# Scores of q as two column tiles of 64 tokens, with k's scores and v's products placed beside them

## The chip, the cores and the metric

The kernel runs on one core of a Trainium2 chip. The metric is device time of one execution in microseconds (us), the median of several runs; a change of about 0.2% (2.2 us) is the least that a measurement of this kernel tells from none.

## What is computed

Agent attention over 12,480 tokens of 128 channels with 49 agents, and behind it two feed-forward layers of width 2048. Everything is float32; the weights of the layers arrive as 64-bit floats and are split into two float32 parts on the chip.

```python
def _attn_ref(q, k, v, agents):
    scale = 1.0 / np.sqrt(q.shape[-1])
    def sm(a, b):
        s = scale * (a @ b.transpose(0, 2, 1))
        s = s - s.max(-1, keepdims=True)
        e = np.exp(s)
        return e / (e.sum(-1, keepdims=True) + 1e-09)
    a2k = sm(agents, k)
    agent_v = a2k @ v
    q2a = sm(q, agents)
    return (q2a @ agent_v).astype(np.float32)
def reference(...):
    x = attn_out.reshape(B * S, D)
    h = x @ w_in;   x = (h / (1 + exp(-h))) @ w_out
    h = x @ w2_in;  return (h * cos(h)) @ w2_out
```

## The kernel before

There are two stages. The **attention stage** goes over 13 blocks of tokens, numbered 0 to 12: twelve of 1024 tokens (128 partitions by 8) and a last one of 192 (96 by 2). The **feed-forward stage** goes over 25 tiles of up to 512 tokens, four groups of hidden channels each.

In the attention stage the order of all work on all engines is written out by hand, in the tables `ORDER` and `FIRST`: a list of steps, each a function and a block number. Every engine takes its own instructions in that order. `qS3` is `qS(3)`, the scores of q for block 3. The steps that matter here:

- `kT`, `qT` (function `turn`, L267): eight transposes of a block of k or q on TensorE into a double bank of PSUM; `kX`, `qX` (L286): ScalarE copies them to an SBUF tile `xT`, of which there are two.
- `kS` (L303): scores of k. The 64 columns of `agk` (49 agents, padded) are the stationary operand, and 512 tokens stream. Two such matmuls stand side by side in the array as column tiles, at `tile_position` (0, 0) and (0, 64). VectorE takes them away in `kM`.
- `qS` (L379): scores of q. Here 128 tokens are the stationary operand, and `agT` streams, the 49 agents twice, 98 columns; the second 49 are written over by the next matmul. Eight matmuls for a block. VectorE then takes the maximum (`qM`, L388), subtracts it (`qB`, L396); ScalarE does the exponential (`qE`), VectorE the sum (`qZ`, L407).
- `qt` (L440): four transposes of half a block of the packed probabilities into the one bank `y2`; `qk` (L445): ScalarE copies that bank to SBUF, and the next `qt` waits for it.
- `vE` (L337, ScalarE): exponentials of k's scores, two blocks at a time; `vt` (L346): their transposes; `vc` (L352): ScalarE's copy; `va` (L366): their product with v, eight matmuls of 49 columns in two column tiles with 128 channels streaming, added up over all blocks in one bank.
- `dA`, `d0` ... `d4`, `dH`, `dL`: the splitting of a piece of weights, on ScalarE (L459, L475) and VectorE (L463 to L498).
- `z0` to `z4`, `c0` ... : after the last `va`, `c0` (L523, VectorE) and `c1` (L526, ScalarE) take the sums away, and a chain of small steps folds them into the first layer's weights. The feed-forward stage starts behind that.

`kS`, `qS` and `vt` share two banks of PSUM (`bank1`), so each of them waits until the one two places ahead of it has been taken away: `kM`, `qB` or `vc`.

Loads of k, q, v and weights are issued by one queue (SP) in the fixed order `LOADS`, each as soon as a buffer of its kind is free (five for k and q, three for v, three for weights); `va` frees v's buffers, `turn` those of k and q, and `d3` those of the weights. A load of 1024 tokens or of a piece of weights is 524,288 bytes.

A float32 matmul that is no transpose shows as two loads and two matmuls in the trace, a transpose as one of each. So `qS` of a full block has 16 matmuls in the trace, `va` 16, `kS` four and `turn` eight.

Of the kernel before, what the change touches and what calls it, by code (L numbers as in the profile page):

```python
# [33 lines left out]


ORDER = """
dA0 d00 d10 kT0 wm3 d20 dH0 d30 kX0 d40 kT1 dL0 kS0 kX1 kT2 kM0 dA1 kS1 kX2 d01 d11 kT3 kM1 dH1 kS2 d21 kX3 d31
kT4 d41 kS3 kM2 kX4 dL1 kT5 dA2 kM3 kS4 kX5 d02 d12 qT0 d22 dH2 d32 kS5 qX0 kM4 kT6 d42 dA3 qS0 kM5 kX6 d03 d13
kT7 dL2 qM0 kS6 kX7 d23 qB0 kT8 dA4 kM6 kS7 kX8 d04 d33 qT1 qE0 d14 dH3 kS8 qZ0 qX1 kM7 kT10 d24 dH4 d43 qS1
kX10 qR0 dL3 qN0 dA5 kM8 kT9 qM1 qP0 qB1 kS10 qK0 qL0 qE1 qT2 kX9 qZ1 d05 qt0.0 qX2 d15 kT11 qR1 d34 qk0.0 qN1  # L40
kS9 dA6 kM10 kT12 d44 kX11 qS2 qP1 kM9 dH5 qK1 d25 qL1 qt0.1 qM2 kS11 qk0.1 qB2 kX12 qt1.0 d35 qE2 qT3 qk1.0 d06
dL4 kS12 qX3 qT4 kM11 d45 dA7 qt1.1 qS3 d16 qX4 d07 kM12 dH6 x0 qZ2 qT5 qk1.1 d17 x1 qR2 qS4 dH7 qM3 qN2 qX5 x2
qP2 qB3 qK2 x3 qT6 qE3 x4 qL2 qM4 vE12 qZ3 qS5 vE0 d26 qR3 dL5 qN3 qX6 qt2.0 qB4 qT7 d27 qE4 qP3 dA8 qZ4 vt1 qK3
qT8 qM5 qk2.0 qL3 qB5 qX7 qt2.1 qR4 d08 qS6 qN4 qk2.1 d36 vc1 qP4 qE5 vt0 vE2 qM6 qT9 qK4 qB6 qL4 qZ5 qt3.0 vc0
d46 va1 qX8 d18 vt3 qk3.0 vt2 d28 vc3 qR5 va0 d37 qN5 vc2 dL6 qE6 qt3.1 va3 qk3.1 qP5 vE4 d47 qT10 qK5 qt4.0 dA9
qZ6 vt4 qL5 dH8 d09 qS7 qk4.0 d38 vc4 dL7 vE8 qt5.0 qS8 qR6 d19 qN6 qk5.0 qM7 dA10 qB7 qt4.1 qX9 d29 vt5 d48 qP6
va2 qk4.1 qM8 qE7 qK6 qB8 va4 qL6 vE6 qZ7 qt5.1 d39 qS9 vc5 dL8 vE10 qR7 d010 qN7 vt6 qM9 qE8 va5 qB9 qP7 vc6 z0
qK7 d110 vt7 dA11 qL7 va6 qk5.1 qZ8 vc7 z1 qt6.0 qX10 z2 d210 vt9 d310 qT11 qk6.0 d011 dH9 d111 qt6.1 qE9 qS10
qR8 d49 qk6.1 qN8 qZ9 dH11 qR9 vc9 qT12 dL9 qP8 qt7.0 dH10 va7 qM10 qX11 qK8 d410 vt10 qN9 qk7.0 va9 qB10 dL10
qE10 qt7.1 qX12 qS11 dA12 qP9 qZ10 qL8 z3 vc10 d012 qk7.1 qK9 vt8 dA13 qM11 qt8.0 qL9 vc8 va10 qB11 qk8.0 d013  # L50
sp0 qS12 qE11 d211 qt9.0 d112 vt11 qk9.0 qR10 va8 z4 qN10 vc11 qM12 qB12 d311 dH12 qt8.1 sp1 vt12 qE12 va11 vc12
qP10 qZ11 qk8.1 qK10 va12 qL10 qt9.1 c0 c1 qZ12 c2 qk9.1 qR12 d411 qN12 c3 qt10.0 c4 c5 st c6 cP0 qP12 d113 cA0
d212 qk10.0 ri0 d312 dH13 d412 qt10.1 cH0 cA1 dL11 qk10.1 dL12 ch0 cl0 cw0 cP3 dA15 cs0 cP2 ch1 d015 cl3 cP1 cH3
cl2 qR11
"""
# [892 lines left out]
```

## Time and profile before

| | |
|---|---|
| time, median of 3 runs | 1079.82 us (1078.44 to 1080.45) |
| span of the profiled execution, first to last instruction | 1076.8 us |
| profiled execution's own time | not listed; the median of the runs is 3.0 us above its span |
| TensorE busy | 1065.2 us, 99% |
| VectorE busy | 964.1 us, 90% |
| ScalarE busy | 909.8 us, 84% |
| GpSimd busy | 504.0 us, 47% |
| HBM read, written | 27.58 MB, 6.39 MB |

The attention stage is the first 94 us, the folding of the sums and the first hidden groups lie between 94 and 146, and the rest is the steady feed-forward stage. A busy TensorE is not one at its peak: matmuls are pipelined, and their durations overlap. What one costs in a row of its kind is read from the chain of work that ended last, which follows starts.

### The profile page before, as it was taken

To read this page: it belongs to the slowest core of one execution; us is meant where nothing else is said; L and a number is where in the kernel's file an instruction comes from. 1 tells how busy PE (TensorE), PEld (TensorE's weight loads), DVE (VectorE), ACT (ScalarE), POOL (GpSimd) and SP (SyncE) were. 2 spreads that over 40 slices of the span, in tenths; PEclk is the share of its full clock that TensorE was granted. 3 is DMA by queue.
4 is the path that set the end of the run, shared out by engine and by line. 5 is a ranking of instruction groups with operands and counts; after the bars stand their busy time and mean duration, and the time that the engine had idled before them with its cause. 6 is when DMAs were issued, how large, how long until landed. Compare 5 with 4: busy or idle time off the path is not lost.

```text
span 1076.8 us, 14174 instructions
## 1 busy us (share of the span) xinstructions
PE 1065.2 (99%) x5267; PEld 841.2 (78%) x5267; DVE 964.1 (90%) x1067; ACT 909.8 (84%) x972; POOL 504.0 (47%) x264
## 2 busy tenths in 40 slices
PE   9999999999999999999999999999999999999997
PEld 5897777777777777777777777777777777788996
DVE  7877999989999999999989998999999999999897
ACT  5888988888888888888888888888888888888876
POOL 0445044554455445544554455445544554455555
PEclk9999999999999999999999999999999999999999
DMA  9963000000000000000000000000000000000000
GB/s 345 344 226 125 9 6 11 6 16 13 4 16 16 1 17 16 1 16 17 10 6 16 12 5 16 13 4 16 17 1 16 16 1 15 15 11 5 12 9 15
DMA packets 66221, 38.68 MB, mean 36 GB/s; under 512 B 52523, under 2 KB 57184, under 8 KB 66152
## 3 DMA queue, kind: packets, MB, share of 16 engines
q1 hardware_dynamic: 65352, 37.68, 11.5%
q8 instruction: 41, 0.67, 0.3%
q14 instruction: 28, 0.23, 0.1%
q10 hardware_dynamic: 800, 0.10, 0.1%
HBM read 27.58 MB, written 6.39 MB: 32 GB/s over the span
## 4 chain that ended last, share of the span: by engine, by line
PE 95%; DVE 2%; ACT 1%; POOL 1%; DMA 1%; issue 1%; SPq 0%; POOLq 0%; DVEq 0%; ACTq 0%
PE y L733 16%; PE y L737 16%; PE y L734 16%; PE h L701 10%; PE h L775 8%; PE h L777 8%; PE h L776 8%; PE h L689 4%; PE h L267 2%; PE h L379 2%; PE h L303 1%; PE y L366 1%; PE y L440 1%; POOL g2l L834 1%; DMA kraw<-in_k_dram 1%; DVE g L816 1%
## 5 line engine op out<-in xcount | busy, mean ns | idle before, releaser
L834 POOL TENSOR_TENSOR g2l<-g,g2h 128x1024 fp32r<-128x1024 f32 (+2 forms) x200 | 465.5, 2349 | 498.7 <-DVE g1l L724 489.0
L799 DVE SCALAR_TENSOR_TENSOR n<-n,h 128x1024 f32<-128x1024 int32 (+3 forms) x202 | 239.0, 1184 | 63.9 <-ACT n L789 50.8
L789 ACT ACTIVATE n<-h,quarter 128x1024 int32<-128x1024 f32 (+3 forms) x202 | 219.8, 1088 | 88.7 <-PE h L777 88.6
L724 DVE TENSOR_TENSOR g1l<-g,g1h 128x1024 fp32r<-128x1024 f32 (+2 forms) x200 | 239.7, 1199 | 9.7 <-ACT g1h L716 4.1
L816 DVE TENSOR_TENSOR g<-n,h 128x1024 f32<-128x1024 f32 (+3 forms) x202 | 238.0, 1179 | 4.0 <-ACT n L808 0.7
L709 ACT ACTIVATE g<-h 128x1024 f32<-128x1024 f32 (+2 forms) x200 | 199.4, 997 | 36.2 <-PE h L701 36.0
L808 ACT ACTIVATE n<-n,halfpi 128x1024 f32<-128x1024 f32 (+3 forms) x202 | 225.6, 1119 | 0.8 <-DVE n L799 0.8
L716 ACT CAST g1h<-g 128x1024 fp32r<-128x1024 f32 (+2 forms) x200 | 204.9, 1025 | 3.2
L825 DVE CAST g2h<-g 128x1024 fp32r<-128x1024 f32 (+2 forms) x196 | 155.5, 794 | 7.5
L733 PE MATMUL y<-g1h,o1h 128*128 128x512 f32 (+2 forms) x400 | 156.4, 391 | 0.1
L733 PE MATMUL y<-g2h,o2h 128*128 128x512 f32 (+2 forms) x400 | 154.9, 387 | 1.1 <-DVE o L856 0.9
L775 PE MATMUL h<-x2h,i2h 128*128 128x512 f32 (+2 forms) x400 | 154.2, 386 | 1.0 <-DVE g L816 1.0
L734 PE MATMUL y<-g2h,o2l 128*128 128x512 f32 (+2 forms) x400 | 154.5, 386 | 0.0
L734 PE MATMUL y<-g1h,o1l 128*128 128x512 f32 (+2 forms) x400 | 154.0, 385 | 0.0
L777 PE MATMUL h<-x2l,i2h 128*128 128x512 f32 (+2 forms) x400 | 153.9, 385 | 0.0
L776 PE MATMUL h<-x2h,i2l 128*128 128x512 f32 (+2 forms) x400 | 153.9, 385 | 0.0
L701 PE MATMUL h<-pT,w2h 128*128 128x512 f32 (+2 forms) x400 | 132.3, 413 | 0.0
L737 PE MATMUL y<-g2l,o2h 128*128 128x512 f32 (+2 forms) x400 | 122.3, 387 | 1.9 <-POOL g2l L834 1.9
L737 PE MATMUL y<-g1l,o1h 128*128 128x512 f32 (+2 forms) x400 | 121.2, 384 | 0.0
L733 PEld LDWEIGHTS y<-g1h,o1h 128*128 128x128 f32 x400 | 75.1, 188 | 21.1 <-DVE x2l L762 7.8
L701 PEld LDWEIGHTS h<-pT,w2h 128*128 128x128 f32 x400 | 67.3, 188 | 30.9 <-issue 23.9
L737 PEld LDWEIGHTS y<-g2l,o2h 128*128 128x128 f32 x400 | 74.9, 188 | 17.7 <-POOL g2l L834 3.1
(140 smaller groups left out, 1092.5 us busy)
## 6 DMA issues: line engine op xcount, KB each, us to landing
...
```

What stands on the lines that cost most here:

```text
L701: nc.tensor.matmul(out=h1s[g, k][:, j, :toks(t)], lhsT=w2h[:, 128 * c:128 * c + 128], rhs=x, start=False, stop=True)
L724: i = v.tensor_tensor(out=gl, in0=f, in1=b32(gh), op=ALU.subtract)
L733: nc.tensor.matmul(out=y, lhsT=wh[:, c, :], rhs=gh[:, j, :], start=(c == 0), stop=False)
L734: nc.tensor.matmul(out=y, lhsT=wl[:, c, :], rhs=gh[:, j, :], start=False, stop=False)
L737: nc.tensor.matmul(out=y, lhsT=wh[:, c, :], rhs=gl[:, j, :], start=False, stop=(c == NCH - 1))
L775: nc.tensor.matmul(out=y, lhsT=i2h[:, c, :], rhs=xh, start=True, stop=False)
L776: nc.tensor.matmul(out=y, lhsT=i2l[:, c, :], rhs=xh, start=False, stop=False)
L777: nc.tensor.matmul(out=y, lhsT=i2h[:, c, :], rhs=xl, start=False, stop=True)
L799: v.scalar_tensor_tensor(out=b32(n)[:, p], in0=n[:, p], scalar=-2.0 * PI, in1=h2s[g, k][:, p], op0=ALU.mult, op1=ALU.add)
L808: sc.activation(out=r[:, p], in_=r[:, p], func=AF.Sin, bias=halfpi)
L816: v.tensor_tensor(out=f[:, p], in0=r[:, p], in1=h[:, p], op=ALU.mult)
L834: i = (v if (g, k) == (NG - 1, 1) else gp).tensor_tensor(out=gl[:, p], in0=f[:, p], in1=b32(gh)[:, p], op=ALU.subtract)
```

## The change

`qS` now makes two matmuls where it made one. Each takes 64 tokens as stationary operand (64 and 32 in the last block) and streams the 49 agents once; the two stand side by side as column tiles at (0, 0) and (0, 64) and write the two halves of the partitions. `agT` holds the agents once, 196 bytes instead of 392, and one copy on VectorE at the start goes. The tiles that are allocated behind `agT` on its side of SBUF (the split weights, `pT`, `g1`, `g1h`, `g1l`, `x2h`, `x2l` among them) begin 192 bytes lower.

```diff
-    agT = const.tile([128, 2, NA], F32, name="agT")
+    agT = const.tile([128, NA], F32, name="agT")
...
-        for j in range(2):
-            nc.vector.tensor_copy(out=agT[:, j, :], in_=pa[:, :NA])
+        nc.vector.tensor_copy(out=agT, in_=pa[:, :NA])
...
             ps = bank1()
-            ag2 = agT.rearrange("p j a -> p (j a)")
             for i in range(n):
-                nc.tensor.matmul(
-                    out=ps[:p, NA * i:NA * i + 2 * NA], lhsT=xt[:, i // h, p * (i % h):p * (i % h) + p], rhs=ag2,
-                    start=True, stop=True,
-                )
+                for x in range(0, p, 64):
+                    w = min(64, p - x)
+                    at = p * (i % h) + x
+                    nc.tensor.matmul(
+                        out=ps[x:x + w, NA * i:NA * i + NA], lhsT=xt[:, i // h, at:at + w], rhs=agT,
+                        start=True, stop=True, tile_position=(0, x),
+                    )
```

The table `ORDER` moves `kS` and `va` steps so that they stand beside `qS` steps. A line of it, before and now:

```diff
-d46 va1 qX8 d18 vt3 qk3.0 vt2 d28 vc3 qR5 va0 d37 qN5 vc2 dL6 qE6 qt3.1 va3 qk3.1 qP5 vE4 d47 qT10 qK5 qt4.0 dA9
+vc3 qR5 va1 va0 d37 qN5 vc2 dL6 qE6 qt3.1 qk3.1 qP5 vE4 d47 qT10 qK5 qt4.0 dA9 qZ6 vt4 qL5 dH8 d09 qk4.0 d38 vc4 dL7
```

The order of the instructions on VectorE, ScalarE, GpSimd and SP stays as it was, but for the one copy; only TensorE's order moves. In the rows below, line numbers of the changed kernel are two lower for `turn`, `kS`, `vt` and `va` (L265, L301, L344, L364).

TensorE around the scores of q for block 1, before: the scores of k (L303) and of q (L379) stand apart, each between transposes.

```order
L267 MATMUL h_427<-ident,qraw 128x128 x8
L303 MATMUL h_445<-xT,agk 64x512 x2
L267 MATMUL h_453<-ident,kraw 128x128 x8
L379 MATMUL h_469<-agT,xT 128x98 x8
L267 MATMUL h_488<-ident,kraw 128x128 x8
```

And now:

```order
L265 MATMUL h_434<-ident,qraw 128x128 x8
L265 MATMUL h_457<-ident,kraw 128x128 x8
L301 MATMUL h_473<-xT,agk 64x512 x2
L379 MATMUL h_476<-agT,xT 64x49 x16
L265 MATMUL h_503<-ident,kraw 128x128 x8
```

The scores of k have moved behind one block of transposes, and those of q follow them at once, as 16 matmuls of 64 by 49.

TensorE from `qt3.1` to `vt5`, before (the rows are `qt3.1`, `va3`, `qT10`, `qt4.0`, `vt4`, `qS7`, `qt5.0`, `qS8`, `qt4.1`, `vt5`):

```order
L440 MATMUL y_891<-ident,pk 128x128 x4
L366 MATMUL y_194<-vraw,eT 49x128 x8
L267 MATMUL h_909<-ident,qraw 128x128 x8
L440 MATMUL y_919<-ident,pk 128x128 x4
L346 MATMUL h_929<-ident,sT 128x128 x4
L379 MATMUL h_937<-agT,xT 128x98 x8
L440 MATMUL y_959<-ident,pk 128x128 x4
L379 MATMUL h_964<-agT,xT 128x98 x8
L440 MATMUL y_984<-ident,pk 128x128 x4
L346 MATMUL h_992<-ident,sT 128x128 x4
```

And now (`qt3.1`, `qT10`, `qt4.0`, `vt4`, `qt5.0`, `va3`, `qS7`, `qS8`, `qt4.1`, `vt5`):

```order
L440 MATMUL y_946<-ident,pk 128x128 x4
L265 MATMUL h_956<-ident,qraw 128x128 x8
L440 MATMUL y_966<-ident,pk 128x128 x4
L344 MATMUL h_976<-ident,sT 128x128 x4
L440 MATMUL y_993<-ident,pk 128x128 x4
L364 MATMUL y_193<-vraw,eT 49x128 x8
L379 MATMUL h_1010<-agT,xT 64x49 x16
L379 MATMUL h_1027<-agT,xT 64x49 x16
L440 MATMUL y_1055<-ident,pk 128x128 x4
L344 MATMUL h_1063<-ident,sT 128x128 x4
```

Between `qt4.0` and `qt5.0`, which share the bank `y2`, only `vt4` is left; `va3` and `qS7` have gone behind them.

TensorE from `vt6` to `qt7.0`, before (`vt6`, `va5`, `vt7`, `va6`, `z1`, `qt6.0`, `vt9`, `qT11`, `qt6.1`, `qS10`, `qT12`, `qt7.0`):

```order
L346 MATMUL h_1056<-ident,sT 128x128 x4
L366 MATMUL y_194<-vraw,eT 49x128 x8
L346 MATMUL h_1082<-ident,sT 128x128 x4
L366 MATMUL y_194<-vraw,eT 49x128 x8
L505 MATMUL h_1106<-rz,both 128x1
L440 MATMUL y_1108<-ident,pk 128x128 x4
L346 MATMUL h_1117<-ident,sT 128x128 x4
L267 MATMUL h_1125<-ident,qraw 128x128 x8
L440 MATMUL y_1139<-ident,pk 128x128 x4
L379 MATMUL h_1145<-agT,xT 128x98 x8
L267 MATMUL h_1164<-ident,qraw 128x96 x2
L440 MATMUL y_1170<-ident,pk 128x128 x4
```

And now (`vt6`, `vt7`, `va5` with `va6`, `z1`, `qt6.0`, `vt9`, `qT11`, `qt6.1`, `va7`, `qS10`, `qT12`, `qt7.0`):

```order
L344 MATMUL h_1135<-ident,sT 128x128 x4
L344 MATMUL h_1151<-ident,sT 128x128 x4
L364 MATMUL y_193<-vraw,eT 49x128 x16
L505 MATMUL h_1185<-rz,both 128x1
L440 MATMUL y_1187<-ident,pk 128x128 x4
L344 MATMUL h_1196<-ident,sT 128x128 x4
L265 MATMUL h_1204<-ident,qraw 128x128 x8
L440 MATMUL y_1218<-ident,pk 128x128 x4
L364 MATMUL y_193<-vraw,eT 49x128 x8
L379 MATMUL h_1232<-agT,xT 64x49 x16
L265 MATMUL h_1259<-ident,qraw 128x96 x2
L440 MATMUL y_1265<-ident,pk 128x128 x4
```

`vt7` has moved up to stand right behind `vt6`, and `va7` has moved up in front of `qS10`; it stood behind `qt7.0`.

## Rows read from the trace of the kernel before

**Rows 1.** The page: its head.

```profile
span 1076.8 us, 14174 instructions
```

**Rows 2.** Windows: stretch, length, busy by engine, granted clock, DMA share, GB/s.

```profile
0.00:9.40 9.40, 7.45 (x30) 4.37 (x30) 4.17 (x23) 3.02 (x5) 0.96 (x10) 1.00 0.72 244
9.40:50.00 40.60, 40.57 (x290) 28.41 (x291) 33.94 (x80) 30.02 (x41) 8.89 (x12) 1.00 1.02 382
50.00:94.00 44.00, 44.00 (x474) 40.12 (x474) 34.98 (x74) 37.25 (x69) 24.03 (x35) 1.00 0.59 203
94.00:108.00 14.00, 12.46 (x80) 9.84 (x80) 11.58 (x26) 12.50 (x22) 4.58 (x9) 1.00 0.26 91
...
146.00:1060.00 914.00, 912.76 (x4179) 722.78 (x4179) 832.39 (x811) 781.58 (x783) 451.44 (x192) 1.00 0.05 11
```

**Rows 3.** Chain of work that ended last, 2 to 74 us: start, length, what.

```profile
2.56 6.83 DMA kraw<-in_k_dram
...
50.91 1.76 PE h L379 x16
...
53.11 0.87 PE h L267 x8
...
59.24 1.01 PE y L366 x16
...
70.61 1.89 PE y L366 x32
72.50 0.59 PE y L440 x4
```

**Rows 4.** TensorE's weight loads in order of time: start, length, line, shape, count.

```profile
20.62 0.14 PEld L303 LDWEIGHTS h<-xT,agk 128*64 128x64 f32 x2 [0.17 <-issue]
...
20.62 0.20 PEld L303 LDWEIGHTS h<-xT,agk 128*64 128x64 f32 x4 [0.17 <-issue]
```

**Rows 5.** The line of kS: its loads' durations in ns, least, median, most.

```profile
L303 PEld LDWEIGHTS h<-xT,agk x52: 132/135/137, 10.5 to 43.4; 128*64 128x64 f32 x52
```

**Rows 6.** TensorE's matmuls in order of time: qT7, qt3.1, vt7, qt6.1, va11 with va12.

```profile
52.95 1.04 PE L267 MATMUL h<-ident,qraw 128*128 128x128 f32 x8
...
62.22 0.66 PE L440 MATMUL y<-ident,pk 128*128 128x128 f32 x4
...
76.23 0.66 PE L346 MATMUL h<-ident,sT 128*128 128x128 f32 x4
...
79.85 0.60 PE L440 MATMUL y<-ident,pk 128*128 128x128 f32 x4
...
92.69 1.30 PE L366 MATMUL y<-vraw,eT 128*49 128x128 f32 x20
```

**Rows 7.** ScalarE in order of time: qk3.1, its next steps, qk4.0; then qk7.0.

```profile
62.91 0.59 ACT L445 CAST pT<-y 128x512 fp32r<-128x512 f32 x1 [0.53 <-PE y L440]
63.39 1.15 ACT L337 ACTIVATE sT<-sT,mk 128x1024 f32<-128x1024 f32 x1
...
65.62 0.58 ACT L445 CAST pT<-y 128x512 fp32r<-128x512 f32 x1
...
83.39 0.61 ACT L445 CAST pT<-y 128x512 fp32r<-128x512 f32 x1
```

**Rows 8.** VectorE in order of time: qM7, qZ7, qM9, qB9; then c0.

```profile
67.58 0.57 DVE L388 TENSOR_REDUCE m<-h 128x8 f32<-128x392 f32 x1
...
71.26 0.57 DVE L407 TENSOR_REDUCE z<-e 128x8 f32<-128x400 f32 x1 [0.24 <-ACT e L402]
...
74.88 0.57 DVE L388 TENSOR_REDUCE m<-h 128x8 f32<-128x392 f32 x1 [1.25 <-PE h L379]
75.56 0.57 DVE L396 TENSOR_TENSOR e<-h,m 128x392 f32<-128x392 f32 x1
...
94.03 0.28 DVE L523 COPY halves<-y 49x128 f32<-49x128 f32 x1 [1.30 <-PE y L366]
```

**Rows 9.** The SP queue: the issue of v7's load (first of two merged).

```profile
76.34 1.93 SPq L210 DMA_DIRECT2D vraw<-in_v_dram  x2
```

More of the change, by code (lines that the diff above doesn't have):

```diff
@@ L36 @@
 ORDER = """
[L37 to L41, printed above, removed]
@@ L42 @@
-dL4 kS12 qX3 qT4 kM11 d45 dA7 qt1.1 qS3 d16 qX4 d07 kM12 dH6 x0 qZ2 qT5 qk1.1 d17 x1 qR2 qS4 dH7 qM3 qN2 qX5 x2
-qP2 qB3 qK2 x3 qT6 qE3 x4 qL2 qM4 vE12 qZ3 qS5 vE0 d26 qR3 dL5 qN3 qX6 qt2.0 qB4 qT7 d27 qE4 qP3 dA8 qZ4 vt1 qK3
-qT8 qM5 qk2.0 qL3 qB5 qX7 qt2.1 qR4 d08 qS6 qN4 qk2.1 d36 vc1 qP4 qE5 vt0 vE2 qM6 qT9 qK4 qB6 qL4 qZ5 qt3.0 vc0
-d46 va1 qX8 d18 vt3 qk3.0 vt2 d28 vc3 qR5 va0 d37 qN5 vc2 dL6 qE6 qt3.1 va3 qk3.1 qP5 vE4 d47 qT10 qK5 qt4.0 dA9
-qZ6 vt4 qL5 dH8 d09 qS7 qk4.0 d38 vc4 dL7 vE8 qt5.0 qS8 qR6 d19 qN6 qk5.0 qM7 dA10 qB7 qt4.1 qX9 d29 vt5 d48 qP6
@@ L47 @@
[L47 to L51, printed above, removed]
@@ L52 @@
-qP10 qZ11 qk8.1 qK10 va12 qL10 qt9.1 c0 c1 qZ12 c2 qk9.1 qR12 d411 qN12 c3 qt10.0 c4 c5 st c6 cP0 qP12 d113 cA0
-d212 qk10.0 ri0 d312 dH13 d412 qt10.1 cH0 cA1 dL11 qk10.1 dL12 ch0 cl0 cw0 cP3 dA15 cs0 cP2 ch1 d015 cl3 cP1 cH3
-cl2 qR11
+dA0 d00 d10 kT0 wm3 d20 dH0 d30 kX0 d40 kT1 dL0 kS0 kX1 kT2 kM0 dA1 kS1 kX2 d01 d11 kT3 kM1 dH1 kS2 d21 kX3 d31 kT4
+d41 kS3 kM2 kX4 dL1 kT5 dA2 kM3 kS4 kX5 d02 d12 qT0 d22 dH2 d32 qX0 kM4 kT6 d42 dA3 kS5 qS0 kM5 kX6 d03 d13 kT7 dL2
+qM0 kS6 kX7 d23 qB0 kT8 dA4 kM6 kS7 kX8 d04 d33 qT1 qE0 d14 dH3 qZ0 qX1 kM7 kT10 d24 dH4 d43 kS8 qS1 kX10 qR0 dL3
@@ new lines @@
+qN0 dA5 kM8 kT9 qM1 qP0 qB1 kS10 qK0 qL0 qE1 qT2 kX9 qZ1 d05 qt0.0 qX2 d15 kT11 qR1 d34 qk0.0 qN1 dA6 kM10 kT12 d44
+kS9 qS2 kX11 qP1 kM9 dH5 qK1 d25 qL1 qt0.1 qM2 kS11 qk0.1 qB2 kX12 qt1.0 d35 qE2 qT3 qk1.0 d06 dL4 qX3 qT4 kM11 d45
+dA7 qt1.1 kS12 qS3 d16 qX4 d07 kM12 dH6 x0 qZ2 qT5 qk1.1 d17 x1 qR2 qS4 dH7 qM3 qN2 qX5 x2 qP2 qB3 qK2 x3 qT6 qE3 x4
+qL2 qM4 vE12 qZ3 qS5 vE0 d26 qR3 dL5 qN3 qX6 qt2.0 qB4 qT7 d27 qE4 qP3 dA8 qZ4 vt1 qK3 qT8 qM5 qk2.0 qL3 qB5 qX7
+qt2.1 qR4 d08 qS6 qN4 qk2.1 d36 vc1 qP4 qE5 vt0 vE2 qM6 qT9 qK4 qB6 qL4 qZ5 qt3.0 vc0 d46 qX8 d18 vt3 qk3.0 vt2 d28
@@ new lines @@
+vc3 qR5 va1 va0 d37 qN5 vc2 dL6 qE6 qt3.1 qk3.1 qP5 vE4 d47 qT10 qK5 qt4.0 dA9 qZ6 vt4 qL5 dH8 d09 qk4.0 d38 vc4 dL7
+vE8 qt5.0 va3 qS7 qS8 qR6 d19 qN6 qk5.0 qM7 dA10 qB7 qt4.1 qX9 d29 vt5 d48 qP6 va2 qk4.1 qM8 qE7 qK6 qB8 va4 qS9 qL6
+vE6 qZ7 qt5.1 d39 vc5 dL8 vE10 qR7 d010 qN7 vt6 qM9 qE8 qB9 qP7 vc6 z0 qK7 d110 vt7 dA11 qL7 va5 va6 qk5.1 qZ8 vc7
+z1 qt6.0 qX10 z2 d210 vt9 d310 qT11 qk6.0 d011 dH9 d111 qt6.1 qE9 va7 qS10 qR8 d49 qk6.1 qN8 qZ9 dH11 qR9 vc9 qT12
+dL9 qP8 qt7.0 dH10 qM10 qX11 qK8 d410 vt10 qN9 qk7.0 qB10 dL10 qE10 qt7.1 qX12 va9 qS11 dA12 qP9 qZ10 qL8 z3 vc10
@@ L55 @@
+d012 qk7.1 qK9 vt8 dA13 qM11 qt8.0 qL9 vc8 va10 qB11 qk8.0 d013 sp0 qS12 qE11 d211 qt9.0 d112 vt11 qk9.0 qR10 z4
+qN10 vc11 qM12 qB12 d311 dH12 qt8.1 sp1 vt12 qE12 va8 va11 vc12 qP10 qZ11 qk8.1 qK10 va12 qL10 qt9.1 c0 c1 qZ12 c2
+qk9.1 qR12 d411 qN12 c3 qt10.0 c4 c5 st c6 cP0 qP12 d113 cA0 d212 qk10.0 ri0 d312 dH13 d412 qt10.1 cH0 cA1 dL11
+qk10.1 dL12 ch0 cl0 cw0 cP3 dA15 cs0 cP2 ch1 d015 cl3 cP1 cH3 cl2 qR11
 """
```

## The prediction

> **What bounds the kernel now.** I read the busy time by stage first, then the chain of work that ended last, then each engine in order of time around the steps that move. The windows [rows 2] say that TensorE is busy without a gap from 9.4 to 94 us (40.57 of 40.60, 44.00 of 44.00), but a busy TensorE proves little, so the chain has to be seen: after one load of k that lands at 9.39, it is an unbroken row of TensorE's blocks up to the end of the attention stage, of which [rows 3] shows the kinds. So every 0.1 us of TensorE before 94 us is on the path as it stands. The second thing to see in [rows 2] is who is close behind: the DMA engines are full until 50 us (share 1.02), and from 50 to 94 ScalarE is busy 37.25 of 44 us and VectorE 34.98. The feed-forward stage, also TensorE's (912.76 of 914), holds the same instructions as before. What the change is worth is therefore by how much sooner `c0` runs, which ends the attention stage and stands at 94.03 [rows 8]. Behind it come the same steps in the same order on all engines, and I let all of it move with `c0`. The span is 1076.8 us [rows 1]; the runs' median, 1079.82, is 3.0 above it, and I carry that over.
>
> **TensorE's work.** Now the eight matmuls of `qS` take 1.76 us, 110 ns for each of 16 [rows 3]. After the change 16 pairs do it. No row shows such a pair, so it is bounded. Below: a pair of `va` streams 128 columns through both tiles, and the second block of a merged `va` costs 1.89 - 1.01 = 0.88 [rows 3], 110 ns for each of 8 pairs; 49 columns would stream in 42. Above: if the weights of the two tiles load one after the other, a pair costs what the 128 columns cost now, 110. Which it is, `kS` tells, whose loads have the same 64 columns: two loads of 132 to 137 ns [rows 5] are over after 0.14 us, so they run side by side, and four after 0.20, so the next pair starts some 55 ns behind the first [rows 4]. I take 55 and 4 for what separates matmuls, 59 ns. `qS` becomes 16 x 59 = 0.94 and saves 0.82; the last block, a quarter, about 0.2. Thirteen blocks: 12 x 0.82 + 0.2 = 10.0 us.
>
> Between column tiles and the whole array there is a price: a block of transposes behind a column block takes 0.59 where four take half of 0.87 [rows 3], so 0.15 more, and the first `va` of a block 0.13 more than the second. `qS` is now a column block too, so this would be paid 13 times more, 3.6 us, if `qS` stood alone; but the order puts `kS` and `va` beside it, and counting the runs of column tiles gives 24 before and 24 now. Net nothing.
>
> The halved `agT` removes one small copy before TensorE waits for k until 9.39 [rows 3]: nothing. That the tiles behind it begin 192 bytes lower I price at nothing, since no row shows a start address to matter; a nanosecond on each of 4179 matmuls [rows 2] would be 4.2 us.
>
> **What is late next, up to 51 us: the loads.** q7 is the 34th load of the fixed order; with it 17.42 MB have been asked for. By 9.4 us 244 x 9.4 = 2.29 MB had moved and by 50 us 382 x 40.6 = 15.51 more [rows 2]. k1 (1.60 MB) landed when 2.29 had moved, so a load is complete some 0.69 MB late; q7's 18.11 MB are there at about 50.8. Loads cannot come sooner with full engines. `qT7` starts at 52.95 now [rows 6]. By then six `qS` have saved 4.9, of which 2.1 can be kept: **`qT7` at 50.8**.
>
> **From 51 us: the short distances.** I follow TensorE's new order with 0.87 for eight transposes, 0.44 for four, 0.88 for a `va`, 0.94 for a `qS`, 0.13 before and 0.15 after a column block.
>
> (a) `qt3.1` comes after three blocks of eight (2.61), six of four (2.64), `qS6`, `va1`, `va0` (2.70) and 0.41 for the blocks: 59.2. Now it is at 62.22, and `qk4.0` ends at 66.20, 3.98 later; ScalarE has no pause between `qk3.1` and it [rows 6, 7], and its order doesn't change. So `qk4.0` ends at 63.2 at the earliest. `qt5.0` needs that bank. Before, `va3` and `qS7` stood between; now TensorE is there at 59.2 + 0.59 + 0.87 + 0.88 = 61.5 and waits 1.7. **`qt5.0` at 63.2.**
>
> (b) `va3` and `qS7` end at 63.2 + 0.44 + 1.01 + 0.94 = 65.6. From the start of `qM7` to the end of `qB9` VectorE needs 76.13 - 67.58 - 0.24 - 1.25 = 7.06 without its two waits [rows 8]: 72.8. `vt7` takes the bank that `qB9` frees, and now stands right behind `vt6`, without `va5` between; TensorE is there 5.83 after `qS7` (`qS8` 0.94, `qt4.1` 0.59, `vt5` 0.44, `va2` and `va4` 1.89, `qS9` 0.94, `qt5.1` 0.59, `vt6` 0.44), at 71.4, and waits 1.5. **`vt7` at 72.9** (now 76.23 [rows 6]).
>
> (c) From `vt7` to `qt6.1` it is 3.62 now [rows 6]; with `va5` among it, and one change of tiles less, 4.35: 77.25. `va7` stands at 77.7, in front of `qS10`. Its load is issued when `va5` has ended, 74.35 (now 76.34 [rows 9], and used 6.4 later). What it takes isn't shown; between nothing and 6.4 us from the issue, `va7` waits 0 to 3.05. A load with full engines took 6.83 [rows 3]; with the share of 0.59 of this stretch [rows 2] I estimate 4.0, a wait of 0.65. `qt7.0` then stands at 80.7. With `va7` and `va9` gone from between, `qt7.1` follows it by `vt10` alone, and needs `qk7.0`: 4.15 after `qt6.1` at the earliest (84.00 - 79.85 [rows 6, 7]), 81.4, and 1.28 after `qt7.0`, which is `qt3.1` to the end of `qk3.1` [rows 6, 7]. **`qt7.1` at 82.0**, after a wait of 0.4.
>
> (d) `qt7.1`, `va9`, `qS11`, `vt8`, `qt8.0`, `va10`, `qS12`: 4.7, so `qt9.0` at 86.7; `qt8.1` again 1.28 behind it (0.25 of it a wait), 87.95; `qt8.1` and `vt12` 0.55; then `va8` 0.88 more than the 1.34 from `va11` to `c0` now [rows 6, 8]. **`c0` at 90.7**, 3.3 sooner. TensorE gives up 10.0 us of work and 6.7 come back as waits. Sum: a span of 1073.5 and a time of **1076.5 us**.
>
> **The rivals.** (1) *The waits don't come*: ScalarE and VectorE have slack of 7 and 9 us in 50 to 94 [rows 2], and may have run further ahead than I let them. Then it is 2.1 up to `qT7` and 5.1 for the seven `qS` behind it: 1072.6. Against it: ScalarE's row in (a) has no gap.
>
> (2) *A pair is no cheaper than 110 ns*, because loads or the issue of twice as many instructions bind; slower than before. Then nothing is saved and the order's waits remain. Through the same steps: `qT7` 52.95, `qt3.1` 62.1, `qt5.0` 66.1, `vt7` 77.1, `qt7.1` 86.3, `c0` 96.1, 2.1 later: 1081.9. It decides from about 91 ns a pair, where the saving only pays the waits. Against it: the loads in [rows 4]. For it: no row has matmuls closer than 55 ns each over 16 of them (`va`, 0.88 [rows 3]), and the change wants 30.
> The Trainium skill has a rule here, in "TensorE: Matmul & The Clock Gate", section "Back-to-back issue gap": a matmul of 1 to 64 columns costs about 25 ns to issue, or about 62 where the sequencer decodes in software. By the first the pair stays at 59 and the sum stands. By the second `qS` would take an estimated 32 x 62 = 1.98 us, 0.22 more than now, and the time would be some 1083.5. The 55 ns of `va` [rows 3] lie below 62 and speak against the second.
>
> (3) *v7 is late*: with 6.4 us from its issue `va7` waits 2.4 longer than I took, a little of which the waits behind it swallow: `c0` at 92.9, 1078.7, no change that can be told.
>
> (4) *Start addresses*: 4.2 us in the feed-forward stage on top of my sum: 1080.7 or more.
>
> A lower clock I don't count: the granted clock was 1.00 (2.4 GHz) in every stretch, also from 94 to 108, where TensorE idled 1.5 of 14 us [rows 2].
>
> **How the numbers follow.** A measurement of this kernel can tell about 0.2%, 2.2 us: faster is below 1077.7, slower above 1082.0. My forecast (1075.2 to 1078.0) has a chance of 0.50, of which 0.44 is faster. Rival 1 has 0.13, faster. Rival 2 has 0.12, half of it slower, since it lies at the bound. Rival 3 has 0.20, of which 0.17 is within and 0.03 faster. Rival 4 has 0.05, 0.04 of it slower. Faster 0.60, within 0.30, slower 0.10. The range goes from rival 1 to just below rival 2: 1072.3 to 1080.5.
>
> **What would show it.** `qS` at 0.94 us a block in the chain, the two tiles' loads starting together. TensorE idle before `qT7`, ended by the load, before `qt5.0` by ScalarE's `qk4.0`, before `vt7` by VectorE's `qB9`, before `va7` by a load. `c0` at 90.7. Wrong it would be if `qS` stays near 1.76, if TensorE still runs without gaps, or if matmuls in the feed-forward stage take other durations than before.

## The result, and the profile after

The changed kernel takes 1085.60 us (median of five, 1083.74 to 1086.11), the kernel before 1078.73 beside it (1078.44 to 1080.45): a ratio of 1.0058, with an interval of 1.0045 to 1.0070. I had forecast 1076.5, faster. It is slower by 6.9 us, which lies outside my range.

In some executions of every kernel here, before's too, TensorE's granted clock is low for a few microseconds somewhere, and these take about 2 us more (before: 1078.4 where the mean clock is 0.999 or 1.00, 1080.0 where it is 0.997 or 0.998); all five of the changed kernel's were such, and "at full clock" below means the median of the other runs of a kernel.

The windows of the changed kernel (columns as in [rows 2]):

```profile
9.40:50.00 40.60, 39.09 (x410) 26.49 (x408) 36.84 (x88) 32.90 (x48) 10.69 (x15) 1.00 1.05 387
50.00:94.00 44.00, 38.95 (x546) 34.74 (x547) 31.43 (x66) 33.88 (x63) 23.11 (x32) 0.96 0.60 202
...
146.00:1060.00 914.00, 913.64 (x4152) 717.29 (x4152) 824.99 (x803) 776.98 (x777) 447.61 (x190) 1.00 0.05 11
```

Three things differ from [rows 2]. TensorE, which had no gap from 50 to 94 us, is now idle for 5 of the 44. Its granted clock there is 0.96. And in the feed-forward stage, where both kernels have the same instructions and TensorE no gap, 914 us hold 4152 matmuls and not 4179.

TensorE's matmuls around the two long gaps (start, length, line, tiles, count; in brackets the idle time ahead and what ended it):

```profile
47.22 1.14 PE L379 MATMUL h<-agT,xT 128*64 128x49 f32 x32
48.29 0.65 PE L440 MATMUL y<-ident,pk 128*128 128x128 f32 x4
50.77 1.16 PE L265 MATMUL h<-ident,qraw 128*128 128x128 f32 x8 [1.82 <-DMA qraw<-in_q_dram]
51.73 1.06 PE L344 MATMUL h<-ident,sT 128*128 128x128 f32 x4
52.58 1.91 PE L265 MATMUL h<-ident,qraw 128*128 128x128 f32 x8
...
81.05 1.08 PE L364 MATMUL y<-vraw,eT 128*49 128x128 f32 x16 [1.56 <-DMA vraw<-in_v_dram]
81.96 1.09 PE L379 MATMUL h<-agT,xT 128*64 128x49 f32 x32
```

`qT7` waits for q7 up to 50.77, as forecast (50.8). Then eight transposes, 1.04 us in [rows 6], take 1.91: the clock. The windows of this place say so, where the third number from the end is the granted clock:

```profile
48.00:50.70 2.70, 0.95 (x18) 0.66 (x13) 2.61 (x6) 2.70 (x6) 2.42 (x4) 1.00 1.01 382
50.70:52.00 1.30, 1.23 (x10) 1.23 (x11) 1.20 (x5) 0.00 (x0) 0.86 (x2) 0.87 0.44 167
52.00:55.50 3.50, 3.50 (x26) 3.24 (x26) 1.06 (x1) 1.20 (x2) 0.60 (x2) 0.56 0.40 129
```

And `va7` waits for v7's load to 81.05. `c0` comes when it came before:

```profile
L523 DVE COPY halves<-y x1: 283/283/283, 94.0 to 94.0; 49x128 f32<-49x128 f32 x1
```

It stood at 94.03 in [rows 8]. So the attention stage gained nothing, where I had 3.3 us, and 6 us were lost behind it. Where behind it, the line of `x2h` tells, which runs once for every four turns of the feed-forward loop (first and last start at the end of each row). This is before:

```profile
L754 ACT CAST x2h<-y x25: 461/589/592, 125.5 to 1046.3; 128x512 fp32r<-128x512 f32 x22, 128x416 fp32r<-128x416 f32 x2, 128x384 fp32r<-128x384 f32 x1
```

and this after:

```profile
L754 ACT CAST x2h<-y x25: 461/587/590, 125.5 to 1052.2; 128x512 fp32r<-128x512 f32 x22, 128x416 fp32r<-128x416 f32 x2, 128x384 fp32r<-128x384 f32 x1
```

Both start at 125.5; the stretch between is 920.8 us before and 926.7 after. I call it **the loop's length**; the loss of 5.9 us lies in it, spread evenly (each 100 us from 250 to 950 hold 447 to 450 matmuls, and 450 to 453 before).

### The profile page after: what moved, and what is told of

It is laid out like the page before. It is cut to its first block, busy times and chain, and to the rows that moved or that the text cites. A ratio compares the mean times of both kernels' runs of the same rounds, so it can differ in the third digit from the quotient of the medians.

```text
span 1082.8 us, 14562 instructions
## 1 busy us (share of the span) xinstructions
PE 1064.5 (98%) x5463; PEld 833.2 (77%) x5463; DVE 961.8 (89%) x1066; ACT 909.7 (84%) x972; POOL 504.2 (47%) x264
## 4 chain that ended last, share of the span: by engine, by line
PE 93%; DMA 2%; DVE 2%; ACT 1%; POOL 1%; issue 1%; POOLq 0%; DVEq 0%; ACTq 0%
PE y L733 16%; PE y L734 16%; PE y L737 16%; PE h L701 10%; PE h L775 8%; PE h L776 8%; PE h L777 8%; PE h L689 4%; PE h L265 2%; DMA qraw<-in_q_dram 2%; PE y L364 1%; PE h L301 1%; PE y L440 1%; PE h L379 1%; POOL g2l L834 1%
## 5 line engine op out<-in xcount | busy, mean ns | idle before, releaser
(140 smaller groups left out, 1074.5 us busy)
```

## Experiments on the feed-forward stage: the addresses

The halved `agT` moved all tiles of the left side by 192 bytes. The first four runs ask whether that, the order or the new scores made the loop longer.

**e1_room_back**: the changed kernel, addresses as before.

```diff
-    const.tile([128, LINE - 8], F32, name="fill")
+    const.tile([128, LINE + 40], F32, name="fill")
```

> The changed kernel with 192 bytes of unused room more behind agT's neighbours, so that every tile of the left side begins at the same address as in the kernel before; order and instructions are those of the changed kernel. Theory A (start addresses): in the changed kernel one turn of the feed-forward loop takes 9.863 us where it took 9.794, and this comes from the 192 bytes. Then the turn is 9.794 again, some 96 turns give back 6 to 6.6 us, and the time is about 1079.2. Theory B (the way in which the engines enter the loop, which the new order has changed, sets where their accesses meet in it): nothing changes, 9.86 a turn and about 1085.6. The attention stage is the same by both: qt9.1 near 93.9.

Measured: 1077.55 us, ratio 0.9987 (0.9979 to 0.9996), and the loop's length is again 920.9. The gain on before is 1.0 us by the medians and 1.6 at full clock, less than the 2.2 us named ahead as the least that can be told, though the interval leaves out 1.

```profile
L754 ACT CAST x2h<-y x25: 456/589/589, 125.7 to 1046.6; 128x512 fp32r<-128x512 f32 x22, 128x416 fp32r<-128x416 f32 x2, 128x384 fp32r<-128x384 f32 x1
```

**e2_shift_before**: the kernel before, left side 64 bytes further on.

```diff
-    const.tile([128, LINE - 8], F32, name="fill")
+    const.tile([128, LINE + 8], F32, name="fill")
```

> The kernel before, old order and old scores of q, with 64 bytes of unused room more in the first pool, so that the tiles of the left side begin 64 bytes off a multiple of 128, as they do in the changed kernel. Theory A (start addresses): a turn of the feed-forward loop goes from 9.794 to about 9.86 us, and the time from 1078.7 to about 1085. Theory B (how the loop is entered): 9.79 and 1078.7.

Measured: 1084.52, ratio 1.0052 (1.0040 to 1.0064); the loop's length is 926.9 without any other change:

```profile
L754 ACT CAST x2h<-y x25: 461/587/590, 125.1 to 1052.0; 128x512 fp32r<-128x512 f32 x22, 128x416 fp32r<-128x416 f32 x2, 128x384 fp32r<-128x384 f32 x1
```

The two together show the cause: unused room gives the 6 us back and takes them. What about the place matters was asked next.

**e7_weights**: in before, the weights and `pT` alone 64 bytes off (`fill` 16 words smaller, and a pool of 16 words between the weights and the activations). **e8_activations**: that pool alone, which moves `g1`, `g1h`, `g1l`, `x2h`, `x2l`.

```diff
+    gap_p = ctx.enter_context(tc.tile_pool(name="gap", bufs=1))
+    gap_p.tile([128, 16], F32, name="gap")
     if True:
         att = ctx.enter_context(ExitStack())
```

> The kernel before, in which the weights and pT alone begin 64 bytes off a multiple of 128; g1, g1h, g1l, x2h, x2l and the raw loads begin at multiples of 128 as before. Theory A1 (the weights' start is what costs: in the changed kernel the matmuls with g2h and g2l, which did not move, became longest, 229.1 to 234.2 ns behind o2l): a turn of 9.86 us, 1084.5. Theory A2 (the start of the activations): 9.794 and 1078.6. Both in part: between.

> The kernel before, in which g1, g1h, g1l, x2h, x2l and the raw loads of q, k and v alone begin 64 bytes off a multiple of 128, and the weights at multiples of 128. Theory A1 (the weights' start): a turn of 9.794 us, 1078.6. Theory A2 (the start of the activations): 9.86, 1084.5.

Measured: 1086.47 (ratio 1.0071, 1.0057 to 1.0084) and 1088.83 (1.0086, 1.0072 to 1.0100); the loop's length 928.6 and 929.8. Both theories fall: each part alone costs more than both together in e2. That pointed to distances between tiles.

**e11_all_shifted**: left and right side both 64 bytes further on, the distances between all large tiles as before.

```diff
-EDGE = 96
+EDGE = 32
...
-    const.tile([128, LINE - 8], F32, name="fill")
+    const.tile([128, LINE + 8], F32, name="fill")
```

> The kernel before with all large tiles of both sides 64 bytes off a multiple of 128: weights, pT, g1, g1h, g1l, x2h, x2l and, on the right side, n, g2, g2h, g2l, x3 and o. Weights and left activations together cost 5.9 us (e2_shift_before), weights alone 8, activations alone 10. Theory R (what counts is that tiles that are in use at the same time begin at the same place of 128 bytes, not where): a turn of 9.794 us and 1078.5. Theory S (each tile that begins off a multiple of 128 costs by itself): 9.86 or longer, 1085 to 1090. Since two parts cost less together than either alone, R is the likelier.

Measured: 1079.13, ratio 1.0002 (0.9993 to 1.0011), the loop's length 920.8:

```profile
L754 ACT CAST x2h<-y x25: 457/589/590, 125.0 to 1045.8; 128x512 fp32r<-128x512 f32 x22, 128x416 fp32r<-128x416 f32 x2, 128x384 fp32r<-128x384 f32 x1
```

So where the large tiles begin does not count here, as long as they move together; their distances do. Four more runs asked between which tiles. In the kernel before: **e13_right_32** moves the right side by 32 bytes (`EDGE = 128`); **e14_o2** puts 16 words ahead of `o2h` and 16 behind `o2l`; **e15_g2** does the same around `g2h` and `g2l`; **e16_o2_g2** does both.

```diff
     for nm in ("o1", "i2", "o2"):
+        if nm == "o2":
+            wts.tile([128, 16], F32, name="ahead")
...
+    wts.tile([128, 16], F32, name="behind")
...
+        pool("gapa", 1, "right").tile([128, 16], F32, name="gapa")
         g2h_p = pool("g2h", 3, "right")
```

> The kernel before with the right side alone (n, g2, g2h, g2l, x3, o) 32 bytes off a multiple of 128, the left side on one. If any difference in the place within 128 bytes costs, 1082 to 1086 (64 bytes between the sides cost 5.9 in e2_shift_before). If only the 64-byte half counts, where 32 bytes off moves the tiles into the other half for part of their lines, half as much or nothing: 1078.5 to 1081.

> The kernel before with the weights o2h and o2l alone 64 bytes off; all else begins at multiples of 128. In e2_shift_before the matmuls of g2h and g2l with them became 2.8, 5.1 and 2.7 ns longer; four of each in a turn are 42 of its 69 ns. Pair theory (a matmul whose moving data and weights begin at different places is the one that is longer): a turn of about 9.837 us, 1082.4, and only the matmuls with o2h and o2l longer. Writer theory (it is the writes of the other engines that meet TensorE's reads): the o2 tiles are written early and only read in the loop, so 9.79 to 9.81 and at most 1080.

> The kernel before with g2h and g2l alone 64 bytes off. Pair theory: the same matmuls as in e14_o2 are longer, 9.837 a turn, 1082.4. Writer theory: g2h and g2l are the tiles that VectorE and GpSimd write beside TensorE's reads of others, so other matmuls than those with g2 become longer too.

> The kernel before with o2h, o2l, g2h and g2l 64 bytes off, all else at multiples of 128. Pair theory: the two move together, so their matmuls are as before: 9.794 a turn, 1078.5. Writer theory: not less than e15_g2.

Measured: 1084.62 (1.0050, 1.0035 to 1.0065), 1092.29 (1.0125, 1.0110 to 1.0140), 1086.96 (1.0074, 1.0057 to 1.0091) and 1089.47 (1.0097, 1.0082 to 1.0112). Already 32 bytes cost. Moving o2 and g2 together does not give it back, but this does not refute the pair theory, because my padding was not clean: the words behind `o2l` moved `pT`, `g1` and `x2` by 128 bytes, those behind `g2l` the output tile `o`, and I had taken 128 for nothing. What speaks against the pair theory as the whole cause is the trace of e15. Two kinds of matmul, before (count, busy us, mean ns):

```profile
L775 PE MATMUL h<-x2h,i2h 128*128 128x512 f32 x340 | 132.5, 390 | 0.0
L737 PE MATMUL y<-g2l,o2h 128*128 128x512 f32 x350 | 108.3, 391 | 0.0
```

and in e15:

```profile
L775 PE MATMUL h<-x2h,i2h 128*128 128x512 f32 x340 | 133.4, 392 | 0.0
L737 PE MATMUL y<-g2l,o2h 128*128 128x512 f32 x350 | 110.0, 395 | 0.0
```

Those that read a moved tile grew by 4 ns, but those of `x2h` with `i2h`, of which neither moved, grew by 2. The writer theory had this for e15; it is not shown by it, since no run moves a writer's tile alone. The last two runs ask for the 128 bytes alone.

**e17_act_128**: as e8, with 32 words. **e18_left_128**: `fill` 32 words larger, the whole left side 128 bytes further on.

> The kernel before with g1, g1h, g1l, x2h, x2l (and the raw loads) 128 bytes further on; every large tile still begins at a multiple of 128. With 64 bytes (e8_activations) this cost 10 us. Theory M (only the place within 128 bytes counts): 9.794 a turn, 1078.6. Theory D (the distance between tiles counts over more than 128 bytes, as e14_o2 and e16_o2_g2 suggest, whose padding also moved these tiles by 128): 9.82 or longer, 1081 to 1092.

> The kernel before with the whole left side 128 bytes further on than the right side; every large tile still begins at a multiple of 128. With 64 bytes (e2_shift_before) this cost 5.9 us. Theory M (only the place within 128 bytes counts): 9.794 a turn, 1078.6. Theory D (the distance between tiles counts over more than 128 bytes): 9.82 or longer, 1081 or more.

Measured: 1090.28 (1.0106, 1.0091 to 1.0121) and 1082.93 (1.0036, 1.0022 to 1.0050): theory M falls. For e17, in which every large tile begins at a multiple of 128 as it did before:

```profile
L757 ACT CAST x2h<-y x25: 461/587/590, 125.4 to 1057.4; 128x512 fp32r<-128x512 f32 x22, 128x416 fp32r<-128x416 f32 x2, 128x384 fp32r<-128x384 f32 x1
```

932.0, 11.2 us longer. All runs of this kind together (all rows are the kernel before but for the moved tiles; "left" is weights and activations; us):

| run | moved against the rest | loop's length | more than before |
|---|---|---|---|
| e11_all_shifted | nothing (all by 64 bytes) | 920.8 | 0.0 |
| e18_left_128 | left by 128 | 925.4 | 4.6 |
| e13_right_32 | right by 32 | 926.0 | 5.2 |
| e2_shift_before | left by 64 | 926.9 | 6.1 |
| e15_g2 | `g2h`, `g2l` by 64, `o` by 128 | 927.9 | 7.1 |
| e7_weights | weights, `pT` by 64 | 928.6 | 7.8 |
| e8_activations | left activations by 64 | 929.8 | 9.0 |
| e16_o2_g2 | o2 and g2 by 64, `pT`, left activations and `o` by 128 | 931.3 | 10.5 |
| e17_act_128 | left activations by 128 | 932.0 | 11.2 |
| e14_o2 | o2 by 64, `pT` and left activations by 128 | 934.5 | 13.7 |

What follows: the distances between the tiles that the loop uses decide, over more than 128 bytes, and each of nine new sets of distances is worse than the old one, by 0.5 to 1.5% of the loop. What stays open is which accesses meet. It is TensorE's matmuls that got longer (a stretch that it fills without a gap holds fewer of them); `x2h`, ScalarE's step in the rows above, did not (median 589 and 587 ns), and neither did VectorE's `g` (mean 1216 ns before and after the change) or GpSimd's `g2l` (2414 and 2411). Against e17, e16 loses no more (10.5 and 11.2) and e14 2.5 us more, so a part of the pair theory may yet hold. And the changed kernel, whose left side went 192 bytes down, loses as much as e2, whose left side went 64 up (5.9 and 6.1); the two differ by 256 bytes, but one such pair does not show that the cost repeats every 256.

The Trainium skill, "SBUF — State Buffer", section "SBUF: two separate sides", says that among the engines only the port pair that VectorE and GpSimd share causes contention, and that TensorE never waits on anyone there. By it all ten runs of the table would have the loop's length of before. Only the one in which no distance changed has it, so here the measurement decides against the page, whatever it is that the distances change.

## Experiments on the attention stage: order, scores, loads

**e3_old_order** (the new `qS` in the order of the kernel before) and **e4_old_scores** (the old `qS`, 98 columns, in the new order), both with the old addresses. With before and e1 they make a square. e3 differs from e1, and e4 from before, in `ORDER` alone.

> The new scores of q alone: the order of the kernel before, the addresses of the kernel before. What the edit of qS is worth without the new order. qS takes 1.0 instead of 1.76 us a block, 10 us in all; standing alone between whole-array work, each of 13 blocks adds a change into and out of column tiles (0.13 and 0.15), 3.6 us. If the waits of the changed kernel are the order's doing, c0 comes 3 to 6 us sooner than 94.0 and the time is 1073 to 1076. If they are those of the loads and of VectorE and ScalarE, which stand in their old order, the gain is used up as in the changed kernel: c0 within 1 us of 94 and 1078 to 1079.

> The new order alone: the old qS with 98 columns (1.76 us a block), the addresses of the kernel before. By the steps of the prediction TensorE has no work less, so the waits that the order brings are added: c0 at 96.1, about 2 us later than before, 1080.8. If TensorE's extra work fills the waits that the changed kernel shows (2 us before qT7, 1.8 before va7), c0 stays near 94.5 and the time near 1079. Theory B (how the loop is entered) would also have the turn of the feed-forward loop at 9.86 here, 1085 or more; theory A leaves it at 9.794.

| | old scores | new scores |
|---|---|---|
| old order | 1078.3 (before, beside them) | 1074.6 (e3) |
| new order | 1082.4 (e4) | 1076.7 (e1) |

These are medians at full clock; over all runs e3 has 1074.86, ratio 0.9959 (0.9947 to 0.9971), and e4 1082.39, 1.0034 (1.0022 to 1.0046). The new scores are worth 3.7 us in the old order and 5.7 in the new one; the new order costs 4.1 with the old scores and 2.1 with the new ones. So the column tiles do what they should, and the order that came with them takes away more than half of it. e3 came as its first theory had it, with `c0` at 90.3, 3.7 us sooner. From 50 to 94 us TensorE has only two waits above 0.3 us there:

```profile
51.20 1.09 PE L266 MATMUL h<-ident,qraw 128*128 128x128 f32 x8 [1.16 <-DMA qraw<-in_q_dram]
...
78.95 1.08 PE L365 MATMUL y<-vraw,eT 128*49 128x128 f32 x16 [0.37 <-DMA vraw<-in_v_dram]
```

e4 came 1.6 us later than its first theory had it (`c0` at 97.8, not 96.1), and its loop's length of 920.9 rules out theory B. TensorE has no work less there than before, yet it waits: its windows row of 50 to 94 us has 40.90 busy where [rows 2] has 44.00.

```profile
50.00:94.00 44.00, 40.90 (x428) 37.37 (x427) 33.05 (x69) 34.68 (x63) 21.80 (x29) 1.00 0.58 196
```

That is the price of the new order by itself: 3.1 us of waits, 0.89 of them for v7's load and the rest at its short distances.

```profile
83.41 1.08 PE L365 MATMUL y<-vraw,eT 128*49 128x128 f32 x16 [0.89 <-DMA vraw<-in_v_dram]
```

Which of its waits it is in the changed kernel, e1 shows, where the clock was at its full level up to 80 us:

```profile
63.08 0.63 PE L440 MATMUL y<-ident,pk 128*128 128x128 f32 x4 [1.00 <-ACT pT L445]
...
72.25 0.66 PE L344 MATMUL h<-ident,sT 128*128 128x128 f32 x4 [0.73 <-ACT eT L350]
...
79.70 1.51 PE L364 MATMUL y<-vraw,eT 128*49 128x128 f32 x16 [2.36 <-DMA vraw<-in_v_dram]
```

The largest is `va7`'s. v7's load takes the buffer that `va5` frees, and `va5` stands later in the new order.

**e5_va5_back**: `va5` ahead of `qB9` again, so that v7 is asked for sooner.

```diff
-... vt6 qM9 qE8 qB9 qP7 vc6 z0 qK7 d110 vt7 dA11 qL7 va5 va6 qk5.1 ...
+... vt6 qM9 qE8 va5 qB9 qP7 vc6 z0 qK7 d110 vt7 dA11 qL7 va6 qk5.1 ...
```

> As e1_room_back (the changed kernel with the old addresses, 1077.55, qt9.1 at 94.1), but va5 stands again ahead of qB9, before vt7, as in the kernel before. In e1_room_back TensorE waited 0.73 before vt7 and 2.36 before va7 for v7's load, which is issued when va5 has ended, and from 80.2 to 83.7 the granted clock was low. Theory (v7 is asked for too late): va5 fills the wait before vt7, v7 is issued some 1.4 us sooner and lands near 78.2; va7 waits about 1.6 us, short of what went ahead of a lower clock so far, and the clock stays at 1.00. qt9.1 at about 90.9, time 1074.3. Rival (the DMA engines are full there, so an earlier issue brings no earlier landing): v7 lands near 79.6 again, va7 waits 3 us, the clock falls again, 1077.5.

Measured: 1077.27, ratio 0.9984 (0.9975 to 0.9993), at full clock 1076.5, which is e1's. The rival holds. In the chain of work, e1's load of v7 (start, length) is

```profile
73.96 5.70 DMA vraw<-in_v_dram
```

and e5's

```profile
72.93 6.70 DMA vraw<-in_v_dram
```

Asked for 1.03 us sooner, it lands at the same time, 79.63 and 79.66. (The steps ahead run 0.35 us later in e5, so measured from them it lands some 0.4 us sooner.) The reason could be read in the kernel before, in narrower windows than mine (this is its own row):

```profile
75.00:80.00 5.00, 5.00 (x59) 4.29 (x58) 3.85 (x10) 4.36 (x8) 1.16 (x2) 1.00 1.03 376
```

The DMA share is 1.03 there, full, where the window of 50 to 94 us has 0.59.

**e9_v7_first**: e1 with v7 ahead of v9 in the order of loads, so that it takes `va4`'s buffer.

```diff
-w9 w10 v2 v4 w11 v5 q12 v6 q11 w12 v9 v7 v10 w13 v8 v11 v12 w15 w14
+w9 w10 v2 v4 w11 v5 q12 v6 q11 w12 v7 v9 v10 w13 v8 v11 v12 w15 w14
```

> As e1_room_back (the changed kernel with the old addresses), but in the order of loads v7 stands ahead of v9. It then takes the buffer that va4 frees and not the one of va5, which stands later in the changed order. Theory (of the attention stage's lost gain the most is v7's load: 2.36 us of wait before va7, where the prediction had 0.65): v7 is asked for near 69.7 instead of 74.5 and is there before TensorE comes to va7 at 76.5 to 77.3; no wait, qt9.1 at 90 to 90.8 (92.5 with the wait and without a lower clock, in e5_va5_back), about 1074.6. Rival (ScalarE and VectorE, not the load, set the end of the stage): their waits take the place of the load's, qt9.1 at 92 or later, 1076 to 1077.

Measured: 1076.44, ratio 0.9976 (0.9966 to 0.9987), at full clock 1075.7.

```profile
77.31 1.08 PE L364 MATMUL y<-vraw,eT 128*49 128x128 f32 x16 [0.26 <-DMA vraw<-in_v_dram]
...
90.53 0.66 PE L440 MATMUL y<-ident,pk 128*128 128x128 f32 x4
```

The wait is 0.26, and `qt9.1`, ahead of `c0`, stands at 90.53, 3.4 us sooner than 93.92 before. The theory holds. The runs' gain at full clock, 2.8, is less. The traced execution itself ends 2.3 sooner (1074.5 and 1076.8), with the clock at 0.50 from 1068 to 1072; no execution of e9 at full clock has a trace, so the rest stays open.

**e12_loads** and **e10_old_order_loads**: e9 and e3, with v7 ahead of v9 and with q7 ahead of q8 and q10.

```diff
-w0 k0 k1 k2 w1 k3 k4 k5 w2 q0 k6 w3 k7 k8 w4 q1 k10 w5 k9 q2 k12 k11 w6 v1 q3 v0 q4 w7 q5 q10 q6 w8 q8 q7 v3 q9
+w0 k0 k1 k2 w1 k3 k4 k5 w2 q0 k6 w3 k7 k8 w4 q1 k10 w5 k9 q2 k12 k11 w6 v1 q3 v0 q4 w7 q5 q6 w8 q7 q8 q10 v3 q9
```

> As e9_v7_first, and q7 ahead of q8 and q10 in the order of loads as well. Theory: TensorE's wait of 1.2 us before qT7 goes too, but ScalarE's chain up to qk4.0 keeps qt5.0 from moving by as much; qt9.1 0.3 to 0.8 sooner than in e9_v7_first, about 1074. Rival: the load order changes nothing behind qT7, since qt5.0 waits for ScalarE anyway: as e9_v7_first. If e10_old_order_loads is still faster than this by over 1 us, it is the new order itself, not its loads, that costs.

> As e3_old_order (the new scores of q in the order of the kernel before, 1074.86), with v7 ahead of v9 in the order of loads, and q7 ahead of q8 and q10. In e3_old_order TensorE waited 1.16 us before qT7 and 0.37 before va7, both for loads. Theory (these two waits are all that is left): qT7 at 50 instead of 51.2, qt9.1 at 88.7 instead of 90.15, 1073.3. Rival (VectorE and ScalarE take up the time gained behind qT7): qt9.1 at 90, 1074.8.

Measured: 1074.50, ratio 0.9962 (0.9950 to 0.9975), and 1074.03, 0.9954 (0.9942 to 0.9967). Both beat both kernels. At full clock e10 is 1.1 faster than e12 (1073.2 and 1074.3), just over the 1 us that was to decide whether the order itself costs, but with three runs each, whose times overlap, they are not told apart. In e12 `qT7` waits no longer:

```profile
48.83 0.66 PE L440 MATMUL y<-ident,pk 128*128 128x128 f32 x4
49.32 1.04 PE L265 MATMUL h<-ident,qraw 128*128 128x128 f32 x8
...
89.80 0.66 PE L440 MATMUL y<-ident,pk 128*128 128x128 f32 x4
```

and `qt9.1` comes at 89.80, 0.73 sooner than in e9, as expected (0.3 to 0.8) and against the rival; the gain over e9 at full clock is 1.3 us. In e10 `qt9.1` comes at 89.58 in the trace, 0.6 sooner than in e3 (90.15) and not 1.5, nearer to the rival's 90 than to the theory's 88.7, since a new wait took the place of the two (ahead of `va6`; the profile names ScalarE's `xT`, which `va6` does not read, so what held it is open):

```profile
72.72 1.08 PE L365 MATMUL y<-vraw,eT 128*49 128x128 f32 x16 [1.73 <-ACT xT L285]
```

**The clock.** In the changed kernel and in e1 the granted clock fell to about half right behind a wait of 2 us. **e6_units** fills the wait before `va7` of e1 with unit matmuls (`wy18` ahead of `va7` in `ORDER`).

> As e1_room_back, but 18 unit matmuls (111 ns each, result unused, in the bank y2) stand ahead of va7, where TensorE waited 2.36 us for v7 and the granted clock then fell to half. v7 lands no sooner by it. Theory (the idle TensorE is what the lower clock follows): granted clock 1.00 from 80 to 85, qS10 0.9 us instead of 1.8, qt9.1 about 1.9 us sooner at 92.2, 1075.6. Rival (the clock falls with what comes behind, many short matmuls in column tiles): the fall stays, 1077.5.

Measured: 1079.82, ratio 1.0010 (1.0001 to 1.0019). The run doesn't decide what I wanted. A unit is two matmuls in the trace, not one, so the filling was twice too long, and `va7` came 2.2 us later than in e1:

```profile
77.71 4.29 PE L273 MATMUL y<-ident 128*128 128x128 f32 x36 [0.68 <-ACT pT L445]
81.92 1.08 PE L364 MATMUL y<-vraw,eT 128*49 128x128 f32 x16
```

At full clock e6 has 1079.7, 3.0 more than e1: whatever holds `va7` is passed on to the end. The question was answered by e5, which waits as long as e1 in the same place. e1's window behind the wait:

```profile
80.20:83.60 3.40, 3.40 (x48) 3.31 (x44) 0.67 (x2) 0.20 (x1) 0.68 (x1) 0.50 0.50 139
```

and e5's:

```profile
80.20:83.60 3.40, 3.16 (x57) 2.78 (x52) 1.88 (x4) 0.88 (x3) 0.38 (x1) 1.00 0.64 179
```

After a wait of 2.36 us the clock was at half (1.2 GHz), after one of 2.44 it stayed at 2.4. So such a wait alone doesn't bring it down. Before, which has no such wait in the attention stage, has the lower clock in a third of its runs too (6 of 17 beside e1; e1 in 6 of 12), but none of these has a trace, and the low stretch need not lie in that stage: in the traces of e12 and e9 it lies behind it (0.68 from 100 to 104 us, 0.50 from 1068 to 1072). That the new order brings it more often, as five of five runs of the changed kernel suggest, is not shown.

## Why the prediction was wrong, point by point

**TensorE's work: right.** A `qS` of 32 matmuls was to take 0.94 us; in the chain of the changed kernel it is 0.92:

```profile
71.72 0.92 PE h L379 x32
```

57 ns a pair, where I had taken 59 from the loads of `kS` and the bounds were 42 and 110. Rival 2 is out. The Trainium skill ("TensorE: Matmul & The Clock Gate", section "Back-to-back issue gap") has about 25 ns for a short matmul, or 62; the trace lies near the smaller figure, with 29 ns a matmul. In the old order (e3) a block is 1.07 up to the next step, 0.15 more, the price that the prediction had for a change from column tiles to the whole array. The square shows 3.7 to 5.7 us of worth, of the 10.0 that I had counted.

**q7, the short distances (a) and (b): right.** `qT7` came at 50.77 (50.8 forecast; 50.28 in e1). In e1, where the clock was full up to there, `qt5.0` is at 63.08 (63.2) and `vt7` at 72.25 (72.9). One name was wrong: `vt7` waited for ScalarE's `vc6`, 0.73 us, not 1.5 for VectorE's `qB9`.

**v7's load: mis-sized.** I took 4.0 us for it, from the DMA share of 0.59 over 50 to 94 us, and a wait of 0.65. It takes 5.70 in e1 and the wait is 2.36: rival 3, whose price I had right (`c0` at 92.9; e5, with the same wait and without the lower clock, has it at 92.6) and whose chance I had too low. The step that failed is the mean over a wide window; the narrow window has 1.03. With v7 taken out of the way in e9, `va7` is at 77.31, where I had 78.35, and `c0` at 90.7, as forecast. That it fits is luck: `va7` comes 1.0 us sooner than I had it, and from there to `c0` it takes 1.0 longer.

**The clock: left out.** I had not counted a lower clock, since the one profiled execution shows 1.00 in each stretch before 1050 us. A single trace says nothing on how often it comes. In the changed kernel it cost about 1.7 us behind 51.7 (from `qT7` to `qt5.0` it takes 14.45 us, 12.80 in e1), of which v7's wait swallowed a part, since v7's load was asked for 2.1 us later than in e1 (76.10 and 73.96) but landed 1.35 later (81.01 and 79.66).

**The addresses: the wrong zero.** "No row shows a start address to matter" was true, and the zero was not: rival 4 happened, with 5.9 us where I had put 4.2 and a chance of 0.05. Two things could have been weighed. The kernel before has two tiles, `fill` and `border`, that nobody reads: it looks as if distances had been set with them. And the stage behind has over 4000 matmuls in a row without a gap, on which a nanosecond each shows.

The sum: the span was forecast at 1073.5 and is 1082.8. Of the 9.3, 6.0 lie behind `c0` (988.8 us from there to the end, and 982.8 before), 5.9 of them in the loop, and 3.3 are `c0`'s own. The latter are the late `va7` (2.7: half of it v7's load, half the lower clock ahead of it) and 0.6 between `va7` and `c0`. So the step that failed by most is the zero for the addresses, and in the attention stage it is the 4.0 us for v7's load.

The 3.0 us that I carried from the span to the time were wrong too. Each execution here takes 1.8 us more than its own span (1078.6 and 1076.8 for before); the other 1.2 came from comparing a traced execution at full clock with a median in which the lower clock had a part.
